# Taking two blocks of the first chunk's second weight half together, and merging a few small TensorE instructions

## The chip, the cores and the metric

One core of one Trainium2 chip. The metric is the device time of one execution, in microseconds (us). A profiled run also gives the span of the trace, about 2 to 3 us shorter than the time. Engines in the profile: PE (TensorE matmuls), PEld (TensorE weight loads), DVE (VectorE), ACT (ScalarE), SP (the engine whose queue issues most DMAs; SPq is that queue, ACTq is ScalarE's). A load has landed when its last data has arrived; a hole is time in which PE could have started the next matmul and did not.

## The reference

An S5 state-space layer and a GELU feed-forward layer, both on the same input `x`, mixed by a gate (T = 2048 rows, D = 640, F = 1728):

```python
g  = sigmoid((x * gate_w).sum(-1, keepdims=True))
Bu = einsum("bld,pd->blp", x, B_bar)              # complex: B_re and B_im
h[t] = Lam_bar * h[t-1] + Bu[t]                   # scan over 2048 steps
a  = 2 * einsum("blp,dp->bld", h, Cmat).real + x * Dskip
b  = gelu(x @ w1 + b1) @ w2 + b2
out = g * a + (1 - g) * b
```

## The kernel before

It works in four chunks of 512 rows. In chunk 0 the weights are still arriving, so its order follows the DMA queue. `w1` is held in two parts for each of the five 128-row pieces `kd` of the contraction: `w1a[kd]`, columns of blocks 0 to 5, and `w1b[kd]`, the rest ("the second weight half"). The loads concerned, in the order of issue on one queue (cuts marked):

```python
load_xn(0, 0, H)
for kd in range(KD):
    nc.sync.dma_start(out=w1a[kd][:], in_=B_w1[kd * P:(kd + 1) * P, 0:cut1])
nc.sync.dma_start_transpose(out=xT[0][:, :, H * P:CH], in_=x2d[H * P:CH, :])
for kd in range(KD):
    nc.sync.dma_start(out=w1b[kd][:, 0:F - cut1], in_=B_w1[kd * P:(kd + 1) * P, cut1:F])
# ... (cut)
nc.sync.dma_start(out=b1x[:, 0:F_LAST], in_=B_b1[F - F_LAST:F]...)       # small
nc.sync.dma_start_transpose(out=BT_re[:], in_=A_B_re[:, :])
nc.sync.dma_start_transpose(out=BT_im[:], in_=A_B_im[:, :])
nc.sync.dma_start_transpose(out=xT[1][:], in_=x2d[CH:2 * CH, :])
# ... (cut: C, w2, later chunks of x)
```

Blocks 0 to 5 of chunk 0 are accumulated together, piece by piece, in six PSUM banks (a bank is the buffer in which TensorE adds up one block). The blocks after them go one by one, each through all five pieces:

```python
def ff1_mm(p, c, kf, kd, t0=0, t1=CH):
    w = w1a[kd][...] if kf < FA else w1b[kd][...]                         # FA = 6
    nc.tensor.matmul(p[:, t0:t1], lhsT=w, rhs=xT[c][:, kd, t0:t1], start=(kd == 0), stop=(kd == KD - 1))

def ff1(c, k0=0):
    for kf in range(k0, KF - 1):
        p = bank()
        # ... (cut)
        for kd in range(KD):
            ff1_mm(p, c, kf, kd)
        ff1_act(p, c, kf)                                                 # GELU on ScalarE
    # ... (cut: the last, narrow block)

# chunk 0
for kf in range(FA):
    ff1_act(banks[kf], 0, kf)
ff1(0, FA)
# ...
ssm(0)
```

`ssm(0)` follows on TensorE: five times an accumulation with `BT_re` and one with `BT_im`, 5 matmuls each.

## Time and profile before

| | before |
|---|---|
| time, median of 3 runs | 218.42 us (218.31 to 218.53) |
| span of the trace | 216.4 us |
| PE busy | 210.8 us, 97% |
| DVE busy | 189.3 us, 87% |

The page's busy time and its chain that ended last (followed back from the end: what each step waited for):

```profile
PE 210.8 (97%) x1361; PEld 128.0 (59%) x1372; DVE 189.3 (87%) x393; ACT 91.8 (42%) x156; POOL 1.6 (1%) x12
...
PE 92%; DMA 4%; SPq 2%; issue 0%; DVE 0%
```

TensorE is the limit: the chain is 92% PE. Only a wait of PE, or columns that it streams, can move the time. Where PE leaves the chain is seen in the chain in order of time (start us, length us, what):

```profile
8.64 5.50 DMA w1b<-in_B_w_dram
14.13 0.05 issue
14.18 4.71 PE bank L268 x21
```

The last `w1b` piece lands at 14.13 us, and from there PE runs without a stop. The timeline of PE from 12.5 us (start us, length us, engine, line, operation, operands, count; in brackets the idle time before and what ended it):

```profile
12.81 1.11 PE L268 MATMUL bank<-xT,w1b 128*128 128x512 bf16 x3
14.18 4.71 PE L268 MATMUL bank<-xT,w1b 128*128 128x512 bf16 x21 [0.27 <-DMA w1b<-in_B_w_dram]
18.72 0.28 PE L284 MATMUL bank<-b1x,ident 128*128 128x65 bf16 x4
18.85 2.32 PE L268 MATMUL bank<-xT,w1b 128*128 128x512 bf16 x10
21.00 0.78 PE L293 MATMUL bank<-w1b,xT 128*128 128x65 bf16 x20
21.62 1.24 PE L473 MATMUL bank<-xT,BT_re 128*128 128x512 bf16 x4
22.69 1.24 PE L473 MATMUL bank<-xT,BT_im 128*128 128x512 bf16 x5
```

And the weight loads in the same stretch:

```profile
12.48 0.42 PEld L268 LDWEIGHTS <-w1b 128*128 128x128 bf16 x3
13.52 0.10 PEld L268 LDWEIGHTS <-w1b 128*128 128x128 bf16 x1 [0.61 <-DMA w1b<-in_B_w_dram]
14.18 0.33 PEld L268 LDWEIGHTS <-w1b 128*128 128x128 bf16 x3 [0.56 <-DMA w1b<-in_B_w_dram]
```

The 0.27 us in brackets understates the loss: the profile gives each matmul 379 ns, but in an unbroken stretch the starts of 512-column matmuls are 216 ns apart. So a hole is read from the starts. The single starts of this first `w1b` block, from the trace (the record of kd=0 is missing; its start is put 216 ns before the next one):

```
piece kd          0       1       2       3       4     next block
start, us      12.590  12.806  13.022  13.523  14.180  14.406
over 216 ns              0       0     0.285   0.441   0.010
```

The holes add up to 0.736 us, and both big ones end when a piece has landed (the last of its landing counts at 13.48 and 14.13 us). Each load posts 16 counts, and PE waits for all of them: of piece 3, 15 counts had come between 11.37 and 12.67 us, and PE went on after the sixteenth. The Trainium skill, "DMA: Bandwidth & Descriptors", section "Why a DMA increments its semaphore by 16 and not by 1", says so too: only the full 16 means that all data has landed.

`BT_re` and `BT_im` are issued one after the other on SP's queue:

```profile
9.59 5.51 SPq L139 DMA_TRANSPOSE BT_re<-in_A_B_re_dram  x1
15.14 4.05 SPq L140 DMA_TRANSPOSE BT_im<-in_A_B_im_dram  x1
```

`BT_im` reached its last landing count at 22.06 us; PE's weight load for it started at 22.48. So before the change it was in time by 0.42 us only.

### The profile page before, as it was taken

What the parts mean: (1) busy time and instruction counts of PE and PEld (TensorE: products, weight loads), DVE (VectorE), ACT (ScalarE), POOL (GpSimd) and SP (SyncE); (2) the same over time, 40 slices, a digit from 0 to 9 for tenths busy, and PEclk for the clock granted to TensorE, in tenths of its full rate; (3) what the DMA queues carried; (4) which work ended last, traced back from release to release, by engine and by line L of the source; (5) the groups of instructions that cost most, each with busy time, mean ns of one, the idle gap of its engine ahead of it and who ended that gap; (6) DMA issues with size and microseconds to landing.
All of it is one profiled execution on the core that took longest, in us unless ns stands there. A gap on an engine that the chain in (4) does not pass through costs nothing.

```text
span 216.4 us, 3467 instructions
## 1 busy us (share of the span) xinstructions
PE 210.8 (97%) x1361; PEld 128.0 (59%) x1372; DVE 189.3 (87%) x393; ACT 91.8 (42%) x156; POOL 1.6 (1%) x12
## 2 busy tenths in 40 slices
PE   7999999999999999999999999999999999999994
PEld 4745444454577775444477777444457777777773
DVE  2889999999989899999999999999999999961152
ACT  3688556675696101556642200456662210022100
POOL 3000000000000000000000000000000000000000
PEclk9999999999999999999999999999999999999999
DMA  5999999995000043000010006100001000100011
GB/s 182 269 223 191 231 206 370 173 260 78 3 0 0 0 132 114 1 0 3 0 24 3 0 0 194 52 2 0 0 3 24 0 3 30 61 33 0 2 61 61
DMA packets 32339, 16.16 MB, mean 75 GB/s; under 512 B 25091, under 2 KB 32324, under 8 KB 32324
## 3 DMA queue, kind: packets, MB, share of 16 engines
q1 hardware_dynamic: 32114, 15.91, 30.1%
q8 instruction: 10, 0.16, 0.3%
q10 hardware_dynamic: 210, 0.04, 0.1%
q14 instruction: 5, 0.04, 0.1%
HBM read 7.24 MB, written 2.62 MB: 46 GB/s over the span
## 4 chain that ended last, share of the span: by engine, by line
PE 92%; DMA 4%; SPq 2%; issue 0%; DVE 0%
PE bank L520 28%; PE bank L268 22%; PE bank L539 20%; PE bank L473 20%; DMA w1b<-in_B_w_dram 3%; DMA xn<-in_A_x_dram 1%; PE bank L293 1%; SPq L127 1%; SPq L125 1%; SPq L124 0%; DVE ot L544 0%; PE bank L284 0%
## 5 line engine op out<-in xcount | busy, mean ns | idle before, releaser
L520 PE MATMUL bank<-w_sb,gel 128*128 128x320 bf16 x448 | 61.6, 299 | 0.0
L520 PEld LDWEIGHTS <-gel 128*128 128x128 bf16 x448 | 43.6, 98 | 17.2
L476 ACT ACTIVATE bu<-bank 128x512 bf16<-128x512 f32 x40 | 23.9, 597 | 41.4 <-PE bank L473 41.4
L272 ACT ACTIVATE gel<-bank,colB 128x512 bf16<-128x512 f32 x52 | 34.8, 692 | 15.7 <-PE bank L268 14.7
L539 PEld LDWEIGHTS <-hs 128*128 128x128 bf16 x330 | 31.8, 98 | 11.9
L429 DVE TENSOR_TENSOR_SCAN g<-r_c,carry,v 128x512 bf16<-128x512 f32 x30 | 37.2, 1272 | 0.0
L523 ACT ACTIVATE gb<-bank,gcol 128x320 f32<-128x320 f32 x32 | 16.5, 526 | 48.2 <-PE bank L520 46.6
L268 PE MATMUL bank<-xT,w1b 128*128 128x512 bf16 x136 | 31.0, 379 | 0.6 <-DMA w1b<-in_B_w_dram 0.3
L268 PE MATMUL bank<-xT,w1a 128*128 128x512 bf16 (+1 forms) x147 | 26.9, 336 | 0.6 <-DMA xT<-in_A_x_dram 0.4
L539 PE MATMUL bank<-CT_re,hs 128*128 128x320 bf16 (+2 forms) x165 | 27.1, 295 | 0.0
L539 PE MATMUL bank<-CT_im,hs 128*128 128x320 bf16 (+2 forms) x165 | 27.1, 295 | 0.0
L544 DVE SCALAR_TENSOR_TENSOR ot<-bank,gcol,gb 128x320 bf16<-128x320 f32 (+2 forms) x33 | 17.4, 535 | 9.5 <-PE bank L539 9.3
L473 PE MATMUL bank<-xT,BT_im 128*128 128x512 bf16 x99 | 24.8, 379 | 0.1
L473 PE MATMUL bank<-xT,BT_re 128*128 128x512 bf16 x97 | 24.7, 379 | 0.2
L268 PEld LDWEIGHTS <-w1b 128*128 128x128 bf16 x140 | 13.5, 98 | 16.9 <-DMA w1b<-in_B_w_dram 1.2
L268 PEld LDWEIGHTS <-w1a 128*128 128x128 bf16 x150 | 14.4, 98 | 12.0 <-issue 0.6
L506 DVE TENSOR_TENSOR bank<-xn,Dbc 128x320 f32<-128x320 bf16 (+2 forms) x33 | 14.3, 483 | 5.7 <-ACT gb L523 5.7
L473 PEld LDWEIGHTS <-BT_im 128*128 128x128 bf16 x100 | 9.8, 98 | 11.8
L473 PEld LDWEIGHTS <-BT_re 128*128 128x128 bf16 x100 | 9.7, 98 | 11.0
L410 DVE TENSOR_TENSOR v<-wa,wb 128x512 bf16<-128x512 bf16 x40 | 15.2, 422 | 0.7
L410 DVE TENSOR_TENSOR wa<-TCOS,g 128x1024 bf16<-128x1024 bf16 x20 | 13.7, 687 | 0.1
L410 DVE TENSOR_TENSOR wb<-TSIN,bu 128x1024 bf16<-128x1024 bf16 x20 | 13.7, 686 | 0.0
(98 smaller groups left out, 130.5 us busy)
## 6 DMA issues: line engine op xcount, KB each, us to landing
out_dram<-ot SPq DMA_DIRECT2D x15, 160.0 KB, 1.8
w_sb<-in_B_w_dram SPq DMA_DIRECT2D x1, 2080.0 KB
xn<-in_A_x_dram SPq DMA_DIRECT2D x3, 640.0 KB, 5.2
w1b<-in_B_w_dram SPq DMA_DIRECT2D x5, 240.0 KB, 4.4
w1a<-in_B_w_dram SPq DMA_DIRECT2D x5, 192.0 KB, 3.3
xn<-in_A_x_dram SPq DMA_DIRECT2D x2, 320.0 KB
Dbc<-in_A_Dskip_dram SPq DMA_DIRECT2D x1, 160.0 KB
out_dram<-ot SPq DMA_DIRECT2D x1, 128.0 KB
```

What stands on the lines that cost most here:

```text
L125: nc.sync.dma_start_transpose(out=xT[0][:, :, H * P:CH], in_=x2d[H * P:CH, :])
L268: nc.tensor.matmul(p[:, t0:t1], lhsT=w, rhs=xT[c][:, kd, t0:t1], start=(kd == 0), stop=(kd == KD - 1))
L272: nc.scalar.activation(out=gel[c][:, kf, :], in_=p[:, :], func=ACT.Gelu_apprx_tanh, bias=b1_c[:, kf:kf + 1])
L410: nc.vector.tensor_tensor(out=o, in0=a, in1=b, op=op)
L429: nc.vector.tensor_tensor_scan(s["g"][:, ri, :], r_c[:, ks:ks + 1].to_broadcast([P, CH]), s["v"][:, ri, :], init, ALU.mult, ALU.add)
L473: nc.tensor.matmul(p[:], lhsT=BT[:, kd, ks * P:(ks + 1) * P], rhs=xT[c][:, kd, :], start=(kd == 0), stop=(kd == KD - 1))
L476: nc.scalar.activation(out=bu[:, ri, :], in_=p[:], func=ACT.Identity)
L506: dve_now(ck.pe, 0.45, lambda: nc.vector.tensor_tensor(out=p[:, 0:d1 - d0], in0=xn[c][:, a, d0:d1], in1=Dbc[:, d0:d1], op=ALU.mult))
L520: nc.tensor.matmul(p[:, 0:d1 - d0], lhsT=gel[c][:m, kf, lo:lo + P], rhs=w2_sb[:m, kf, d0:d1], start=(kf == 0), stop=(kf == KF - 1))
L523: nc.scalar.activation(out=gb[:, d0:d1], in_=p[:, 0:d1 - d0], func=ACT.Identity, scale=gcol[:, 1, ti:ti + 1])
L539: nc.tensor.matmul(p[:, 0:d1 - d0], lhsT=hs[c][:, j, lo:lo + P], rhs=CT[:, j % KS, d0:d1], start=False, stop=(j == 2 * KS - 1), skip_group ...
L544: nc.vector.scalar_tensor_tensor(out=ot[:, d0:d1], in0=p[:, 0:d1 - d0], scalar=gcol[:, 0, ti:ti + 1], in1=gbs[ti][:, d0:d1], op0=ALU.mult, ...
```

## The change

The intent: with two blocks interleaved, PE has two matmuls for each `w1b` piece instead of one while the pieces trickle in. Besides, the four bias matmuls of the last narrow block become one with a repeated operand, and two warm-up matmuls become one of the same total width.

```diff
-    for _ in range(2):
-        nc.tensor.matmul(wps[:, 0:P], lhsT=warm[:, 0:P], rhs=warm[:, 0:P], start=True, stop=True)
+    nc.tensor.matmul(wps[:, 0:2 * P], lhsT=warm[:, 0:P], rhs=warm[:, 0:2 * P], start=True, stop=True)
 ... (cut)
         if c == 0:
-            for a in range(TPC):
-                nc.tensor.matmul(pv[:, a, :], lhsT=ident[:], rhs=b1x[:], start=(a == 0), stop=True, skip_group_check=True)
+            nc.tensor.matmul(pv, lhsT=ident[:], rhs=b1x[:].rearrange("p (o n) -> p o n", o=1).to_broadcast([P, TPC, NL]),
+                             start=True, stop=True, skip_group_check=True)
 ... (cut)
-    ff1(0, FA)
+    two_banks = [bank(), bank()]
+    for kd in range(KD):
+        for i in range(2):
+            ff1_mm(two_banks[i], 0, FA + i, kd)
+    for i in range(2):
+        ff1_act(two_banks[i], 0, FA + i)
+    ff1(0, FA + 2)
```

## The prediction

> **What bounds the kernel now.** TensorE. The page's first part has PE busy 210.8 us of a 216.4 us span (97%), VectorE 87%, ScalarE 42%. The chain that ended last is 92% PE: DMA issue and w1b landing up to 14.13 us, then an almost unbroken run of PE pieces to 213.4 us. So the time moves only if PE waits less or streams fewer columns.
>
> **The wait aimed at.** The timeline of single instructions at 12.5 to 14.5 us shows the first block that reads w1b, one accumulation over five kd pieces. Unhindered 512-column matmuls start 216 ns apart. Here kd=2 starts at 13.022, kd=3 at 13.523, kd=4 at 14.180, the next block at 14.406. The weight loads of kd=3 and kd=4 start right after their pieces landed (13.48 and 14.13). Lost: 0.285 + 0.441 + 0.010 = 0.74 us. (The view of waits prints 0.3 us for PE, because the modelled 379 ns of a matmul covers part of the hole.) The Trainium skill, "TensorE: Matmul & The Clock Gate", section "Step-by-step: what each phase is for", says matmuls stay in program order and only weight loads are pulled ahead; the trace agrees: the ready matmuls of the next block stand behind kd=3 and kd=4.
>
> **What the change does.**
> 1. Two blocks interleaved by kd: six matmuls, not three, stand before kd=3. From 12.59 us, 6 x 0.216 takes PE to 13.89 (piece 3 landed 13.48) and 8 x 0.216 to 14.32 (piece 4 landed 14.13). Both waits vanish, the second with 0.19 us to spare. The pair ends near 14.75 rather than 15.49: -0.74 us. Two banks must be free at 12.59: the second block's waits on VectorE's last reads of the transposed parameters, done at 11.9; the third block's on the first GELU (13.6). Neither binds.
> 2. Four 65-column bias matmuls become one of 260. They take 18.723 to 18.846 = 0.123 us; 260 columns at 216/512 ns each are 0.110. Gain 0.01 us.
> 3. Two 128-column warm-up matmuls become one of 256: same columns, and PE waits afterwards for xn (3.86 us) and xT (9.10 us). Gain 0.
>
> **What is given back.** PE then reaches the first BT_re matmul at about 20.87 instead of 21.616 and BT_im at 21.95 instead of 22.694. BT_im lands completely only at 22.06 us; its load was issued 15.14 to 19.19 in a queue that does not depend on PE. So PE should stop until about 22.11: a new wait of about 0.17 us. Net shift: about -0.58 us.
>
> **Does it survive?** The slacks I read exceed 0.6 us: hs of chunk 0 is complete at 72.40, first wanted near 74.2 (its first part, 72.06, at 73.5); seeds lead by over 3 us; other loads land many us early. VectorE is busy from 26 us on and will not move before fin_a(0), where it waits for PE, so later pieces shift together. The tail is PE-bound.
>
> **Prediction:** 218.42 - 0.6 = 217.8 us, range 217.35 to 218.25. Faster by over 2%: 1%. Within 2%: 98%. Slower: 1%.
>
> **What would show it:** matmuls 216 ns apart from 12.6 to 14.7 with no w1b wait; a new PE wait of 0.1 to 0.3 us on BT_im near 22 us; one bias matmul of about 0.11 us spacing; later PE pieces about 0.58 us earlier; span near 215.8.
>
> **What would make it wrong:** other landing times (w1b piece 4 later than 14.3 brings part of the wait back; BT_im earlier gives the full 0.75); a bank not free at 12.6; a tight VectorE handover in fin_a; a slow repeated-operand matmul.

## The result, and the profile after

The time was 218.07 us, median of 6 runs (217.73 to 218.29), against 218.38 for the kernel before in the same session (6 runs, 217.90 to 219.07). The ratio is 0.9983, with a 95% interval of 0.9966 to 1.0001. (A ratio here is the mean time of one kernel's fast runs over that of the other's in the same rounds, so it is not quite the ratio of the medians.) The medians differ by 0.31 us, the traces by 0.2 us of span. The predicted 217.8 us, 217.35 to 218.25, holds the measured time. That range is 0.9 us wide and "no change" (218.38) lies only 0.13 us outside of it, so the hit alone says little for the mechanism; the traces and the experiments below have to.

The page after:

```profile
PE 211.9 (98%) x1368; PEld 128.2 (59%) x1368; DVE 189.8 (88%) x393; ACT 91.7 (42%) x156; POOL 1.6 (1%) x12
...
PE 88%; SPq 5%; DMA 5%; issue 0%; DVE 0%
```

PE's timeline in the same stretch:

```profile
12.84 5.56 PE L267 MATMUL bank<-xT,w1b 128*128 128x512 bf16 x25
18.24 0.28 PE L282 MATMUL bank<-b1x,ident 128*128 128x260 bf16 x1
18.36 2.32 PE L267 MATMUL bank<-xT,w1b 128*128 128x512 bf16 x10
20.51 0.78 PE L292 MATMUL bank<-w1b,xT 128*128 128x65 bf16 x20
21.13 1.24 PE L478 MATMUL bank<-xT,BT_re 128*128 128x512 bf16 x5
22.49 1.25 PE L478 MATMUL bank<-xT,BT_im 128*128 128x512 bf16 x5
```

All 25 matmuls before the bias one are now one piece: no hole at `w1b`. But the five `BT_re` matmuls start at 21.13 and the first `BT_im` one at 22.49, 1.366 us later by the trace's single starts; five matmuls need 1.078. This is a new hole of 0.288 us. The view of waits shows no such wait for PE, since the modelled 379 ns cover it again, but it does for the weight loads:

```profile
PEld L478 <- DMA BT_im<-in_A_B_im_dram: 0.6, 1, 0.6
```

The chain in order of time no longer goes through `w1b`. It now goes through the issue of the `BT_re` load and the `BT_im` load behind it, which landed at 22.45 us:

```profile
9.85 5.63 SPq L139
15.48 0.04 issue
15.52 6.92 DMA BT_im<-in_A_B_im_dram
22.45 0.05 issue
22.49 9.89 PE bank L478 x45
```

The sum of the two traces, from the first `w1b` matmul to the first `BT_im` matmul, accounts for the whole difference:

| step | before to after, us |
|---|---|
| PE reaches the first `w1b` matmul (12.590, 12.844) | +0.254 |
| the holes at `w1b` | -0.736 |
| bias matmuls, start to the next start (0.123, 0.115) | -0.008 |
| the hole at `BT_im` | +0.288 |
| sum | -0.202 |
| measured at the first `BT_im` matmul (22.694, 22.493) | -0.201 |

From there on the two executions are the same. From the first `BT_im` matmul to the last matmul of the kernel it is 190.437 us before and 190.448 us after. (In every other trace with this order of accumulations it is also 190.437 to 190.448, the longer where there was a hole: the second matmul after a late weight load comes 226 ns after the first, not 216.) So whatever the change does, it does before 22.5 us; nothing is lost or won further down.

The first line of the table does not come from the `w1b` blocks. TensorE's clock opened to full speed 4.97 us after the start of the span in the trace of before, and 6.95 us in that of after; until then matmuls take about twice as long (256-column ones start 213 ns apart, afterwards 109). The windows view shows it as fewer matmuls per microsecond (columns: window, length, then busy time and count of PE, PEld, DVE, ACT and POOL, and so on). Before, then after:

```profile
5.00:6.00 1.00, 1.00 (x11) 0.82 (x10) 0.64 (x4) 0.59 (x2) 0.00 (x0) 1.00 0.73 243
6.00:7.00 1.00, 1.00 (x12) 0.90 (x10) 0.90 (x5) 0.74 (x2) 0.00 (x0) 1.00 0.99 230
```

```profile
5.00:6.00 1.00, 1.00 (x7) 0.66 (x6) 0.59 (x4) 0.59 (x2) 0.00 (x0) 1.00 0.88 229
6.00:7.00 1.00, 1.00 (x7) 0.69 (x6) 0.90 (x5) 0.69 (x2) 0.00 (x0) 1.00 0.90 272
```

That cost 0.83 us of PE's time. Of it, 0.57 us vanished in a wait for the transposed half of x, which the trace of before has until 9.1 us and that of after has not, and 0.25 us arrived at `w1b`. It went no further: the first `BT_im` matmul starts when `BT_im` has landed, and the chain above ties that landing to SP's queue and not to PE, so an earlier PE would only have waited longer there.

### The profile page after: what moved, and what is told of

Read it like the earlier page. It is cut to its first block, busy times and chain, and to the rows that moved or that the text cites. A ratio compares the mean times of both kernels' runs of the same rounds, so it can differ in the third digit from the quotient of the medians.

```text
span 216.2 us, 3470 instructions
## 1 busy us (share of the span) xinstructions
PE 211.9 (98%) x1368; PEld 128.2 (59%) x1368; DVE 189.8 (88%) x393; ACT 91.7 (42%) x156; POOL 1.6 (1%) x12
## 4 chain that ended last, share of the span: by engine, by line
PE 88%; SPq 5%; DMA 5%; issue 0%; DVE 0%
PE bank L525 28%; PE bank L544 20%; PE bank L478 20%; PE bank L267 19%; DMA BT_im<-in_A_B_im_dram 3%; SPq L139 3%; DMA xn<-in_A_x_dram 1%; SPq L127 1%; SPq L125 1%; PE bank L292 1%; SPq L124 0%; SPq L138 0%; DVE ot L549 0%
## 5 line engine op out<-in xcount | busy, mean ns | idle before, releaser
L267 PE MATMUL bank<-xT,w1a 128*128 128x512 bf16 (+1 forms) x150 | 27.6, 344 | 0.0
L267 PEld LDWEIGHTS <-w1a 128*128 128x128 bf16 x150 | 14.9, 100 | 11.7
L415 DVE TENSOR_TENSOR wb<-TSIN,g 128x1024 bf16<-128x1024 bf16 x20 | 13.7, 684 | 0.0
```

The source lines that it names most:

```text
L415: nc.vector.tensor_tensor(out=o, in0=a, in1=b, op=op)
```

## The experiments

Theory A: PE in chunk 0 is held by one landing after the other. The change takes away the `w1b` holes (0.74 us), but PE cannot start `BT_im` before it has landed, so part of the gain turns into a wait there, and how much differs from run to run with the landing. Theory B, in its several forms: the interleave gives less than it seems, or the gain is lost further down (VectorE, PSUM banks), or the merged instructions matter. All kernels gave correct results. Each was timed in 5 rounds, with the kernel before run 11 times beside each group on the same chip. Runs e1 to e4 were one group (before: 218.26), e5 to e8 the second (before: 218.09), e9 to e11 the third (before: 218.19).

| run | median us | ratio to before (95%) | hole at `BT_im` in its trace, us |
|---|---|---|---|
| e1, interleave alone | 217.60 | 0.9970 (0.9936 to 1.0004) | none |
| e2, change + reordered SSM start | 217.59 | 0.9962 (0.9933 to 0.9990) | none |
| e3, before + reordered SSM start | 218.30 | 1.0000 (0.9967 to 1.0032) | none |
| e4, merged instructions alone | 218.31 | 0.9993 (0.9963 to 1.0023) | none |
| e5, change, `BT_im` late | 222.50 | 1.0181 (1.0139 to 1.0222) | 3.41 |
| e6, before, `BT_im` late | 221.75 | 1.0165 (1.0127 to 1.0204) | 2.47 |
| e7, change, bias load on the other queue, early | 218.16 | 0.9994 (0.9965 to 1.0023) | none |
| e8, change again | 217.53 | 0.9968 (0.9941 to 0.9994) | 0.30 |
| e9, change, bias load on the other queue, later | 217.94 | 0.9995 (0.9981 to 1.0009) | none |
| e10, as e2 | 217.54 | 0.9969 (0.9954 to 0.9985) | none |
| e11, change, third time | 217.83 | 0.9983 (0.9968 to 0.9997) | 0.33 |

### e1 and e4: the parts alone

e1 has only the third part of the diff above; e4 has only the first two parts.

> The two-block interleave alone, bias and warm-up matmuls as before. Theory A (the w1b waits go, then PE stops at BT_im until it has landed): the same as the full change, 0.2 to 0.4 us under before; in the trace no hole at w1b, and a hole of 0.1 to 0.5 us before the first BT_im matmul, which starts within 0.1 us of BT_im's last landing count. Theory B (the gain comes from fewer instructions, the interleave does nothing): within 0.1 us of before.

> The two merged instructions alone (bias 4 to 1, warm-up 2 to 1), no interleave. Theory A: 0.01 us, so within 0.1 us of before; the merged bias matmul occupies 0.11 to 0.12 us to the next start against 0.123 us for the four. A side question: does the full clock open later with the merged warm-up (it opened about 2 us later in the profile of the changed kernel than in that of before)? If the merge does that, it does so here too.

The interleave alone gave 217.60 us against 218.26, the merged instructions alone 218.31. In e1's trace the `w1b` hole is gone:

```profile
12.80 5.56 PE L268 MATMUL bank<-xT,w1b 128*128 128x512 bf16 x25
...
21.09 1.25 PE L479 MATMUL bank<-xT,BT_re 128*128 128x512 bf16 x5
22.17 1.24 PE L479 MATMUL bank<-xT,BT_im 128*128 128x512 bf16 x5
```

In e4's trace it is there:

```profile
12.93 1.03 PE L267 MATMUL bank<-xT,w1b 128*128 128x512 bf16 x4
14.58 4.71 PE L267 MATMUL bank<-xT,w1b 128*128 128x512 bf16 x21 [0.62 <-DMA w1b<-in_B_w_dram]
19.12 0.28 PE L282 MATMUL bank<-b1x,ident 128*128 128x260 bf16 x1
```

By single starts it is 0.79 us, this time nearly all before the last piece. So the gain belongs to the interleave. (The traces say so; of the times, e1's interval reaches 1.0004. But all six timings with the interleave and the loads in their old order, the result and e1, e2, e8, e10 and e11, lie 0.31 to 0.67 us under before, and e3 and e4, without it, within 0.05 us of it.) Two parts of my expectation of e1 failed: the gain, 0.66 us, was above the 0.2 to 0.4 us expected, and its trace has no hole at `BT_im`. There `BT_im` had landed at 21.49 us, before PE's weight load at 21.95. The landing is not a constant.

The side question of e4: the full clock opened at 7.12 us there, with the merged warm-up, but at 6.87 us in e1, where the warm-up is unmerged. Over all traces the opening lay at 3.87, 4.93, 4.97 and 6.87 us with two warm-up matmuls, and between 3.95 and 7.12 us with the merged one (one trace has no record). The ranges overlap, so the late opening in the first trace of after is not shown to come from the merge; a small shift can't be excluded from so few.

### e2 and e3: wanting `BT_im` 1.08 us later

In chunk 0 the SSM's first four accumulations are put in the order re0, re1, im0, im1, on top of the change (e2) and of the kernel before (e3):

```diff
-        for ks in range(KS):
-            bu = work.tile(...)
-            for ri, BT in enumerate((BT_re, BT_im)):
+        order = [(ks, ri) for ks in range(KS) for ri in range(2)]
+        if c == 0:
+            order[0:4] = [(0, 0), (1, 0), (0, 1), (1, 1)]
+        for ks, ri in order:          # bu[ks] made at its first use; scan_ops(ks) after ri == 1
```

> The full change, and in chunk 0 the SSM's first four accumulations in the order re0, re1, im0, im1, so BT_im is wanted 1.08 us later. Theory A: the BT_im hole disappears and the whole of the w1b wait is kept, 0.6 to 0.8 us under before (ratio about 0.997) and 0.3 to 0.5 us under the full change; no PE hole over 0.05 us after 9.5 us. Theory B (the rest of the 0.74 us was lost further down, in VectorE or bank handovers): no better than the full change.

> The kernel before with the same re0, re1, im0, im1 order alone. Theory A: before has no BT_im wait (landed 0.4 us ahead of its weight load), so this gives nothing: within 0.1 us of before, the two w1b holes still there. Rival (the order of the accumulations is itself cheaper, e.g. through ScalarE): 0.3 us or more under before.

e2 came to 217.59 us and e3 to 218.30: the order alone gave nothing (its trace still has 0.75 us of holes at `w1b`), and with it in both, the change is worth 218.30 - 217.59 = 0.71 us, the size of the `w1b` holes (six runs each; I estimate some 0.6 us of uncertainty either way from their scatter). PE's timeline of e2 has no hole from the first `w1b` matmul on:

```profile
12.77 5.56 PE L267 MATMUL bank<-xT,w1b 128*128 128x512 bf16 x25
...
21.05 2.32 PE L484 MATMUL bank<-xT,BT_re 128*128 128x512 bf16 x10
23.21 2.32 PE L484 MATMUL bank<-xT,BT_im 128*128 128x512 bf16 x10
```

But `BT_im` had landed at 21.41 us in that run, so this very trace would have had no hole in the old order either, and e1, in the old order and the same group, was as fast (217.60 us). So e2 does not yet show that the new order gains anything. That is why e2 was run again, beside the change itself.

### e10 and e11: the same, in the same rounds as the change

> e2 once more, in the same rounds as the full change (e11). Theory A: 0 to 0.4 us under e11 (the hole at BT_im, which was 0.29, 0.30 and none in the three profiles with the interleave so far), and 0.5 to 0.8 us under before; no hole at BT_im.

> The full change, third time: 0.2 to 0.6 us under before; a hole at BT_im of 0 to 0.5 us.

e10 took 217.54 us and e11 217.83. The intervals of their ratios overlap, so the times alone don't settle the 0.3 us between them. The traces say where it lies. The change has the hole, by single starts 0.325 us:

```profile
20.89 1.24 PE L478 MATMUL bank<-xT,BT_re 128*128 128x512 bf16 x4
22.30 1.25 PE L478 MATMUL bank<-xT,BT_im 128*128 128x512 bf16 x5 [0.16 <-DMA BT_im<-in_A_B_im_dram]
```

e10 has none (one record of its first ten is missing; its `BT_im` starts 2.158 us after `BT_re`, and ten matmuls need 2.157):

```profile
21.00 2.32 PE L484 MATMUL bank<-xT,BT_re 128*128 128x512 bf16 x9
23.16 2.32 PE L484 MATMUL bank<-xT,BT_im 128*128 128x512 bf16 x10
```

PE came to `w1b` 0.13 us later than in e11, and yet the last matmul of e10 started at 212.513 us against 212.744.

### e5 and e6: `BT_im` landing about 3 us later

```diff
-    nc.sync.dma_start_transpose(out=BT_im[:], in_=A_B_im[:, :])
     nc.sync.dma_start_transpose(out=xT[1][:], in_=x2d[CH:2 * CH, :])
+    nc.sync.dma_start_transpose(out=BT_im[:], in_=A_B_im[:, :])
```

> The full change with the load of BT_im put behind that of xT[1], so that BT_im lands about 3 us later (near 25 us). Theory A (PE cannot pass BT_im's landing, whatever it gained before): PE stops at the first BT_im matmul for about 3 us until the landing; about 2.5 us over before, and within 0.15 us of e6, which has the same late BT_im without the change: the change is worth nothing there. Theory B (the gain at w1b is kept whatever comes after): 0.6 us or more under e6.

> The kernel before with the same late BT_im. Theory A: the two w1b holes are still there (0.7 us), then a hole of about 2.3 us at BT_im; about 2.5 us over before, the same as e5 within 0.15 us, since both go on from the same landing.

The change (e5), then before (e6):

```profile
21.12 1.24 PE L478 MATMUL bank<-xT,BT_re 128*128 128x512 bf16 x5
25.61 1.25 PE L478 MATMUL bank<-xT,BT_im 128*128 128x512 bf16 x5 [3.24 <-DMA BT_im<-in_A_B_im_dram]
```

```profile
14.73 4.71 PE L268 MATMUL bank<-xT,w1b 128*128 128x512 bf16 x21 [1.29 <-DMA w1b<-in_B_w_dram]
...
22.16 1.25 PE L473 MATMUL bank<-xT,BT_re 128*128 128x512 bf16 x5
25.71 1.25 PE L473 MATMUL bank<-xT,BT_im 128*128 128x512 bf16 x5 [2.31 <-DMA BT_im<-in_A_B_im_dram]
```

e5 reaches `BT_re` 1.04 us earlier than e6 (21.12 and 22.16) and starts `BT_im` 0.1 us earlier (25.61 and 25.71), each 0.05 us after its landing (25.56 and 25.67): nearly all of the lead became a longer wait. Spans are 219.3 and 219.4 us. In the timed runs the two can't be told apart (ratios 1.0181 and 1.0165, intervals overlapping), and the change is not ahead; the intervals are too wide to exclude 0.6 us, so it is the traces that speak against theory B. Three things were off. The holes at `w1b` in e6 were 1.47 us, not 0.7: its last piece landed at 14.69 us. The cost in the traces was 2.9 us over the first trace of before, not 2.5, and in the timed medians 3.7 to 4.4 us: both kernels had some runs of 220.0 to 221.5 us of span beside those near 219. The record has a sign of why: the mean granted TensorE clock was 0.991 or 0.992 in exactly those seven runs (four of e5, three of e6) and 0.998 or 0.999 in the five near 219. By my estimate from these figures, 0.7% of 220 us is 1.5 us of full-speed clock, against 1.4 to 1.9 us of longer span. Where in the run the clock was lower, and why, stays open, as no trace of such a run was taken. Split by that clock (after the fact), the mean times are 220.95 us (e5) and 221.11 us (e6) at the higher and 222.82 and 222.62 us at the lower: within 0.2 us either way.

### e8: the change once more

> The full change once more, beside the others and before, to see how much the landing of BT_im moves from run to run: 0.2 to 0.6 us under before; the hole at BT_im between 0 and 0.5 us, and equal to the landing time minus the time at which PE arrives (near 22.0 to 22.2 us).

217.53 us, 0.56 us under before. PE came to `BT_im` at 21.97 us, `BT_im` had landed at 22.22, and the first matmul started at 22.268: a hole of 0.301 us. With the first trace and e11, three traces of the change gave holes of 0.288, 0.301 and 0.325 us.

### e7 and e9: `BT_im` issued earlier, two misses

The small bias load `b1x` (16 KB) stands before the `BT` loads in SP's queue and takes 0.43 us to issue. e7 issues it from ScalarE's queue at 3.65 us; e9 from the same queue after ScalarE's last sine, at 10.62 us.

```diff
-    nc.sync.dma_start(out=b1x[:, 0:F_LAST], in_=...)
+    nc.scalar.dma_start(out=b1x[:, 0:F_LAST], in_=...)      # e7: same place; e9: after the last Sin
```

> The full change with the small b1x load issued from the other DMA-issuing queue, so that the two BT loads are issued about 0.45 us earlier. Theory A: BT_im lands about 0.45 us earlier (near 21.6 us), the hole at BT_im is 0.1 us or less in the trace, and the time comes to that of the reordered version of the first group, 0.6 to 0.8 us under before. Rival (that version won by its order, not by BT_im being in time): no better than the full change beside it.

> e7 mended: there the b1x load, issued at 3.7 us, came among the first weight loads and PE lost 0.9 us before the w1b blocks (waits on w1a and xT), so the verdict was confounded. Here the b1x load is issued by ScalarE's queue only after its last sine (near 11 us), with the early loads as in the full change. Theory A: BT_im is issued about 0.45 us earlier and lands near 21.6 us, the hole at BT_im is at most 0.1 us, PE starts w1b at 12.5 to 12.9 as in the full change, and the time equals that of e10 within 0.15 us and is not above that of e11. Rival (order, not landing): as e11 or worse.

Both did what was meant to `BT_im` (landed at 21.06 and 22.03 us, no hole there) and both lost it elsewhere, so neither tests the theory cleanly. e7:

```profile
7.89 1.48 PE L267 MATMUL bank<-xT,w1a 128*128 128x256 bf16 x12 [0.54 <-DMA w1a<-in_B_w_dram]
9.74 2.12 PE L267 MATMUL bank<-xT,w1a 128*128 128x256 bf16 x18 [0.37 <-DMA xT<-in_A_x_dram]
```

The early small load went out with the first weights: the fourth `w1a` piece landed at 7.85 us, against 6.55 to 7.16 in the other twelve traces, and x's half at 9.70 against 8.64 to 9.19. PE started `w1b` at 13.24 us. This fits the Trainium skill, "DMA: Bandwidth & Descriptors", section "Issuing engines are not separate DMA queues": loads issued by different engines run on the same 16 DMA engines and interleave. e9:

```profile
18.70 0.27 PE L281 MATMUL bank<-b1x,ident 128*128 128x260 bf16 x1 [0.77 <-ACT gel L270]
```

Here PE stood 0.94 us before the bias matmul (single starts: 17.546 and 18.697). The releaser named is wrong. ScalarE's bank had long been free, and PE's own queue was in a wait on `b1x`, whose last landing count came at 18.56 us, 7.9 us after its issue, together with the `BT_re` load (landed 18.79 us), which was being issued at the time. As rivals they do show one thing: removing the hole at `BT_im` gains nothing if another landing then comes too late.

## Why the prediction was right, and what was off in it

- "From 12.59 us ... Both waits vanish ... -0.74 us": right. In the first trace the holes went from 0.736 us to none, and e2 against e3, where nothing takes it back, gave 0.71 us. The spare on the last piece was thinner than the 0.19 us I gave: in the first trace its weight load waited until 14.560 us and its matmul started on time at 14.571; in e11 it came 0.018 us late.
- "Four 65-column bias matmuls become one ... 0.01 us": right, 0.123 to 0.115 us, and e4 shows no more. "Warm-up ... Gain 0": nothing found (e4), with the clock's opening left open.
- "A new wait of about 0.17 us" at `BT_im`: the mechanism was right and shown by e5, e6 and the three traces of the change: in all five the first `BT_im` matmul starts 0.046 or 0.047 us after the last landing count. The size was the mis-sized term: 0.29, 0.30 and 0.33 us in those three. I took the landing from one trace, 22.06 us. Over the traces with the load in its old place it came between 21.41 and 22.72 us; it was at 22.45, 22.22 and 22.25 in the three. That the first hole, 0.288 us, still fell within the 0.1 to 0.3 us that I had named was partly luck: `BT_im` landed 0.39 us later than in the trace of before, but PE came 0.25 us later too. With PE on time the hole would have been 0.54 us.
- "Net shift about -0.58 us": 0.31, 0.56 and 0.36 us between medians in three sessions, and 0.20 us between the two first traces. Between the traces the whole shortfall is the landing: PE started `BT_im` at 22.49 us, 0.05 us after it had landed, and not at 22.11. PE's later start at `w1b` (clock, 0.25 us), which I had not counted, only made the wait shorter. What the shortfall in the timed runs is made of, the traces don't tell.
- "Does it survive": right. From `BT_im` on the traces are alike to 0.01 us over 190 us.
- The bound behind it all: the change can gain no more than the time by which the next landing was early. In the trace of before, PE started `BT_im` at 22.694 us, and could have started at about 22.06 + 0.05 = 22.11: 0.58 us, less than the 0.74 us at `w1b`. (The 0.42 us of slack above is counted to the weight load, which there starts 0.21 us before its matmul. After a late landing it starts only 0.005 us before: 22.488 and 22.493 us in the trace of after.)

The change with the reordered SSM start (e2, e10) stands at 0.9962 and 0.9969 of before. That it beats the change itself is not shown by the times: its lead in the same rounds is 0.29 us of medians, inside the noise, and e1 and e8, in the old order, came to 217.60 and 217.53 us. The traces show the hole gone.

## What to carry to other kernels

When the start of a kernel is a chain of landings, a removed wait is worth at most the slack of the next landing: list the landings with the times at which the engine will want them after the change, before counting the gain. Read that slack from several traces, because landings move by more (here 1.3 us) than such a gain. Changing the order in which data is wanted cost nothing that the runs show (e3), while shifting a load to another queue moved the wait to another load both times (e7, e9).

## What the Trainium skill lacked or had wrong

- "TensorE: Matmul & The Clock Gate", section "Back-to-back issue gap": it gives about 131 ns as the sustained spacing of 512-column matmuls with weight loads, and about 81 ns for 128 columns. Here 512 columns were 216 ns apart in every unbroken stretch, each with its own weight load, and 65 columns about 29 to 35 ns. The section's formula for an isolated gap (N/2.4 + 2.5 ns, 216 for 512) fits; its sustained figure for 512 columns doesn't, and no stretch here measures the one for 128.
- The same page, section "What's actually happening": the clock's opening is said to vary by about 500 ns (and, further down, to be run-variable). Over the traces here it lay between 3.87 and 7.12 us after the start of the span, while the first matmul started at 1.18 to 1.19 us in each.
- No page that I found tells the restart after a late weight load: the next matmul came 226 ns after the one that had waited, not 216.
- "DMA: Bandwidth & Descriptors", section "DMA Transpose (X-bar)": the pages have bandwidths for transposed loads, but I found no time to landing. Here `BT_im`, 640 x 640 bf16, took the issuing queue 3.6 to 4.3 us (`BT_re`, of the same size and issued before it, 5.2 to 6.1 us) and landed 6.3 to 7.2 us after its issue began, between 21.4 and 22.7 us over the traces with the old order of loads.
- The same page, section "Latency and other measured facts", gives about 2 us of fixed cost for a DMA. A 16 KB load behind large ones landed 5.3 us after its issue (9.11 to 14.38 us, before) and 7.9 us (e9): it was in flight together with `w1b` loads of 240 KB each and the `BT_re` load, which probably set its time; no run separates this.
